# Key features turned by VectorE and moved within SBUF, in place of transposes on TensorE

## The chip, the cores and the metric

The kernel runs on one core of a Trainium2 chip. The metric is the device time of one execution in microseconds. Before the change three runs took 670.96 to 671.16 us, with a median of 671.12 us. One further execution was recorded by the hardware profiler; the profile's numbers come from that one.

The core has five engines that run side by side, each through its own queue and in that queue's order: TensorE (PE in the profile; its weight loads are listed as PEld), VectorE (DVE), ScalarE (ACT), GpSimd (POOL) and SyncE (SP). SyncE and GpSimd issue the DMAs here. Data lie in SBUF, and TensorE's results in PSUM, which has eight banks.

## The reference

A sequence of 2048 rows of width 448 is normalised (`xn`) and goes two ways; the result is `x + A(xn) + B(xn)`. B is a gated feed-forward layer with 1792 inner columns. A is attention with 16 heads of width 28, in four blocks of 512 rows, with a memory that is carried from block to block:

```python
for s in range(N):                                   # N = 4 blocks
    qs, ks, vs = q[:, :, s], k[:, :, s], v[:, :, s]
    p = _softmax(qs @ ks^T * scale + mask)           # within the block
    a_dot = p @ vs
    pq = phi(qs)                                     # phi(t) = t + 1 if t > 0 else exp(t)
    o = g * (pq @ M) / (pq @ z + 1e-6) + (1 - g) * a_dot
    pk = phi(ks)
    M = M + pk^T @ vs                                # per head, 28 x 28
    z = z + sum of pk over the rows
```

So the answer that the memory gives to a block's queries needs the key features (`pk`) and values of all blocks before it. The memory after the last block isn't needed.

## The kernel before, in words

The program has a front and a main part. The front, up to about 140 us, normalises the rows and computes keys, queries, values and the memory's answers, block by block. The main part runs feed-forward products on TensorE with the attention of 16 units woven between them, and then the output projection.

Within the front each block `b` does the following.

- *Values.* Four products `pv`, one for each 128 rows (`values`, L400; eleven matmuls of 448 columns each). ScalarE copies each into the tile `vst` (`store_values`, L395), where each head has 28 columns of values and 4 columns of ones; the ones give `z`. After the fourth, `vst` is stored to DRAM (`vd`).
- *Seven key and query steps* (`keys_queries`, L407): the 896 columns of keys and queries lie in seven chunks of 128, the keys in chunks 0 to 3 (the fourth has 64 of keys and 64 of queries). Eleven matmuls make `pp`, with features in the partitions and the block's 512 rows in the columns. ScalarE copies it to `qk` and makes two activations into the feature tile `e`; VectorE makes the low part of `qk` and finishes `e` (L424). SyncE stores `qk` to DRAM (`qd`, L420) and, from the fourth chunk on in blocks 1 to 3, the query features `e` to DRAM (`fd`, L427). The tiles `e` come from a ring of four (`bufs=4`).
- *Key features by row* (`key_rows`, L430): the update sums over rows, so it needs rows in the partitions. TensorE transposes each key chunk of `e` in four pieces into `pk`, and ScalarE copies it to `kn`. This stands after the fourth step (chunks 0 and 1) and after the sixth (chunks 2 and 3).
- *The update* (`update`, L438), right after the seventh step: for each head and each of four groups of 128 rows a matmul with 28 columns of `kn` stationary and 32 columns of `vst` streaming, added up in the bank `pmm`. Four heads at a time use four column strips of the array. Four VectorE operations add the sums to the memory `mst`. Blocks 0, 1 and 2 make an update.

In blocks 2 and 3 the answers to the queries of the block before are made. `load_features` (L459, four DMAs) brings the query features back from `fd` into the tile `phi`, of which there is one. `recall` (L462) multiplies the memory with them; this stands inside the first step in block 2 and inside the second in block 3. VectorE turns the result into a work tile `ts`: in block 2 that is `phi` itself, in block 3 `kn`. Then `answer` (L475), once for each of four groups, makes four VectorE operations and a DMA on GpSimd's queue. In block 2 the answers stand in steps 2, 3, 4 and 7.

Rows of blocks 2 and 3 are normalised by VectorE (`normalise`, L348) during the values of the block before, turned in pieces of 32 by 32 into a staging place (`stage_of`: the room of `phi` for block 2, of `acc[2]` for block 3), and sent to their partitions by 16 DMAs (`spread`, L368, half on SyncE and half on GpSimd). `split_strips` (L377) then makes operands of them in steps 3 to 6.

PSUM banks come from small rings by tag: two "p", two "s", one "m", two "gu", one "pd" (L124). Both the values and the even chunks of keys and queries use "p"; a new tile takes the bank of the one before last and waits until it has been read.

The order of TensorE, ScalarE and VectorE in the front is the order of the code (`manual_schedule(engines=FRONT)`). The queues of SyncE and GpSimd are put in order by a planner, which issues what its own estimate says is ready, and by the order of the code among what is ready.

## Time and profile before

| | |
|---|---|
| median of three runs | 671.12 us |
| profiled execution, its own time | 671.5 us |
| its span (first to last instruction) | 669.6 us |
| PE busy | 663.7 us, 99% of the span |
| DVE busy | 571.4 us, 85% |
| ACT busy | 336.1 us, 50% |
| POOL busy | 147.4 us, 22% |
| chain that ended last | PE 97%, DVE 2% |
| transposes of key features (pk, L434) | 48 |
| update products (pmm, L445), two passes each | 384 passes |

The granted clock of TensorE was full in the whole span. A row of a group reads: line, engine, operation, what it writes and reads, form, count, then total busy time and mean duration in ns of one, then the idle time before it and what ended it. A row of the timeline reads: start, duration, engine, line, operation, and in brackets idle time before it with what ended it. Matmuls are pipelined, so a row's duration overlaps the next row; what an instruction holds of TensorE's queue is read from one start to the next. For SyncE (SPq) a row is the issuing of a DMA, not its transfer.

### The profile page before, as it was taken

Reading aid. Unit: us, or ns where it says so; the run is one execution under the profiler, and the core shown is the slowest. Engines: PE = TensorE matmul, PEld = TensorE weight load, DVE = VectorE, ACT = ScalarE, POOL = GpSimd, SP = SyncE. Lnnn points to the kernel's source line nnn. Section 1 sums busy time; section 2 is a strip of 40 time slices with the busy share of each in tenths; the row PEclk is TensorE's granted clock in tenths of the full one; section 3 lists DMA queues with packets and bytes.
Section 4 is the critical chain, followed back from the end, with each engine's and each line's share of the span. In section 5 each row is a group of like instructions: output and inputs, shape, how many; then the busy total and the mean of one; then the engine's idle time right before and its main releaser. Section 6 shows DMA issues by size and latency. Waiting matters only on the chain.

```text
span 669.6 us, 11201 instructions
## 1 busy us (share of the span) xinstructions
PE 663.7 (99%) x3922; PEld 553.2 (83%) x3922; DVE 571.4 (85%) x987; ACT 336.1 (50%) x560; POOL 147.4 (22%) x354
## 2 busy tenths in 40 slices
PE   8999999999999999999999999999999999999997
PEld 7888888778888888788787878788887887888897
DVE  6986695878999899899998999899998997999864
ACT  4848474423556455455645546455544644545220
POOL 3502210002222222233122322222122122321000
PEclk9999999999999999999999999999999999999999
DMA  8537788995523432324243423426243352323442
GB/s 321 221 128 251 238 287 284 309 273 197 144 73 88 109 93 73 103 57 105 74 96 103 89 72 57 128 52 141 57 103 64 92 115 57 86 78 80 112 153 97
DMA packets 48767, 88.09 MB, mean 132 GB/s; under 512 B 6856, under 2 KB 22856, under 8 KB 48200
## 3 DMA queue, kind: packets, MB, share of 16 engines
q1 hardware_dynamic: 45048, 79.01, 39.1%
q0 software_dynamic: 3520, 8.26, 6.1%
q8 instruction: 31, 0.51, 0.3%
q14 instruction: 24, 0.20, 0.1%
q10 hardware_dynamic: 144, 0.11, 0.0%
HBM read 52.89 MB, written 32.64 MB: 128 GB/s over the span
## 4 chain that ended last, share of the span: by engine, by line
PE 97%; DVE 2%; DMA 0%; ACT 0%; issue 0%; DVEq 0%
PE pgu L260 42%; PE pd L184 21%; PE pp L412 11%; PE st L704 6%; PE pa L790 5%; PE po L889 5%; PE pv L392 5%; PE pk L434 1%; PE pmm L445 1%; PE n L467 1%; DMA acc<-in_x 0%; DVE stats L324 0%; PE pt L103 0%; DVE xn L350 0%; DVE xs L110 0%
## 5 line engine op out<-in xcount | busy, mean ns | idle before, releaser
L260 PE MATMUL pgu<-xs,wgu 128*128 128x512 f32 x1232 | 301.2, 392 | 0.0
L260 PEld LDWEIGHTS pgu<-xs,wgu 128*128 128x128 f32 x1232 | 228.7, 188 | 46.6 <-issue 2.5
L184 PE MATMUL pd<-wdn,hh 128*128 128x448 f32 x672 | 155.3, 366 | 0.0
L184 PEld LDWEIGHTS pd<-wdn,hh 128*128 128x128 f32 x672 | 122.7, 188 | 11.6 <-issue 0.8
L719 POOL TENSOR_SCALAR_AFFINE_SELECT w<-w 128x256 f32<-128x256 f32 (+1 forms) x160 | 76.1, 479 | 224.0 <-ACT w L708 157.6
L772 ACT ACTIVATE w<-w 128x1024 f32<-128x1024 f32 (+1 forms) x96 | 87.8, 915 | 58.3 <-DVE w L768 58.1
L708 ACT ACTIVATE w<-st 128x512 f32<-128x512 f32 x128 | 75.6, 592 | 60.1 <-PE st L704 59.8
L768 DVE TENSOR_TENSOR w<-w,mb 128x1024 f32<-128x1024 f32 (+1 forms) x96 | 100.6, 1054 | 0.8
L726 DVE TRANSPOSE_TENSOR_REDUCE mx<-w 128x32 f32<-128x1024 f32 x64 | 78.9, 1233 | 4.9 <-POOL w L719 4.9
L412 PE MATMUL pp<-xs,wqk 128*128 128x512 f32 x308 | 73.7, 393 | 0.2 <-DVE kn L473 0.2
L186 DVE TENSOR_TENSOR acc<-pd,acc 128x448 f32<-128x448 f32 x112 | 67.4, 602 | 4.0 <-PE pd L184 4.0
L283 ACT ACTIVATE hh<-sg 128x512 fp32r<-128x512 f32 x56 | 35.3, 631 | 67.7 <-DVE sg L277 44.6
L412 PEld LDWEIGHTS pp<-xs,wqk 128*128 128x128 f32 x308 | 57.2, 188 | 12.9 <-issue 0.8
L704 PE MATMUL st<-qk 84*128 84x128 f32 (+3 forms) x256 | 62.0, 313 | 0.0
L267 ACT ACTIVATE sg<-pgu 128x512 f32<-128x512 f32 x56 | 33.2, 592 | 45.0 <-PE pgu L260 44.9
L704 PEld LDWEIGHTS st<-qk 84*128 84x128 f32 x256 | 47.9, 189 | 8.7 <-issue 1.4
L277 DVE SCALAR_TENSOR_TENSOR sg<-sg,pgu 128x512 f32<-128x512 f32 x56 | 37.7, 673 | 10.1 <-PE pgu L260 9.9
L754 DVE STREAM_TRANSPOSE mb<-top 128x1024 f32<-128x1024 f32 x32 | 39.5, 1234 | 3.3 <-POOL top L751 3.2
L286 DVE SCALAR_TENSOR_TENSOR hh<-sg,hh 128x512 fp32r<-128x512 f32 x56 | 38.2, 681 | 0.2 <-ACT hh L283 0.2
L419 DVE TENSOR_TENSOR qk<-pp,qk 128x512 fp32r<-128x512 f32 x28 | 19.2, 686 | 22.2 <-ACT e L417 21.6
L790 PE MATMUL pa<-w,vv 128*32 128x128 f32 (+3 forms) x512 | 37.8, 436 | 0.0
L392 PE MATMUL pv<-wv,xs 128*128 128x448 f32 x176 | 37.4, 367 | 0.3 <-POOL wv L508 0.2
(113 smaller groups left out, 607.2 us busy)
## 6 DMA issues: line engine op xcount, KB each, us to landing
qk<-qd SPq DMA_DIRECT2D x192, 112.0 KB
qd<-qk SPq DMA_DIRECT2D x28, 512.0 KB
raw<-in_w_ffn SPq DMA_DIRECT2D x14, 512.0 KB
acc<-in_x SPq DMA_DIRECT2D x5, 896.0 KB
vd<-vst SPq DMA_DIRECT2D x4, 1024.0 KB
vv<-vd SPq DMA_DIRECT2D x16, 256.0 KB
od<-w POOLq DMA_DIRECT2D x16, 256.0 KB, 4.1
sums<-od SPq DMA_DIRECT2D x32, 128.0 KB
```

Of the source, the lines that this page charges most:

```text
L184: T.matmul(pd[:, :D], l, r, start=n == 0, stop=n == len(mms) - 1)
L186: V.tensor_add(acc[b][:, t, :], pd[:, :D], acc[b][:, t, :])
L260: T.matmul(dst, wgu[f][:, w, side * P:(side + 1) * P], xs[b][:, a, :], start=n == 0, stop=n == len(TERMS) - 1)
L392: T.matmul(pv[:, :D], xs[b][:, a, t * P:(t + 1) * P], wv[w], start=n == 0, stop=n == len(TERMS) - 1)
L412: T.matmul(pp, wqk[c][:, w, :], xs[b][:, a, :], start=n == 0, stop=n == len(TERMS) - 1)
L704: T.matmul(st[:, at:at + L - kb * P], self.qk[:KS, 1, h, kb * P:(kb + 1) * P], self.qk[:KS, 0, h, kb * P:], start=True, stop=True)
L708: A.activation(w, st, AF.Copy)
L719: G.affine_select(d, d, pattern=pattern, base=0, channel_multiplier=-1, compare_op=ALU.is_ge, fill=MASK)
L726: V.tensor_reduce(self.mx[:, 32 * h:32 * h + 32], w3[:, h, :2 * L].rearrange("p (b n) -> p b n", n=32), axis=mybir.AxisListType.X, op=ALU. ...
L768: V.tensor_sub(w, w, m)
L772: A.activation(w, w, AF.Exp, scale=SCALE)
L790: T.matmul(pa[32 * j:32 * j + 32, kb * P:], self.vv[:, kb, 32 * j:32 * j + 32], self.pairs[j // 2].block(j % 2, kb), start=kb == 0, stop=k ...
```

## The change

In blocks 1 and 2 the key features are no longer transposed by TensorE. VectorE transposes each 32 by 32 piece where it is (`turn_keys`), into a staging place, and 24 DMAs within SBUF carry the pieces to their partitions in `kn` (`send_keys`). The staging place is that of the next block's rows: the room of `phi` in block 1, `acc[2]` in block 2. The fourth chunk, of which only half is keys, is turned into another tile of the ring "e". Chunk 0 is turned in step 2, chunks 1 and 2 in step 3, with 16 DMAs after them, and the fourth in step 4, with 8. Block 0 keeps its transposes.

The updates of blocks 1 and 2 move into the next block, after its second value product. The first two value products wait with their copies to `vst` until the update has read it, and the third uses a bank "s".

The update's operands change places in all blocks: `vst` (32 columns) is stationary, and `kn` streams. In blocks 1 and 2 `kn` is laid out in pieces of 32 features, so that a head of 28 features streams one piece or two: 32 or 64 columns. The memory is kept transposed in a new tile `memory`, with six VectorE operations and a transpose into `mst` per update.

In block 2 only the first answer to block 1's queries stays, in step 2. The other three move into block 3, one after each of its first three value products. `phi` is loaded for block 3 after the fourth value product, no longer at the block's start.

```diff
+EXCHANGED = (1, 2)
...
         def values(b, t):
-            pv = bank("pv", "p")
+            late_update = b - 1 in EXCHANGED
+            pv = bank("pv", "s" if late_update and t == 2 else "p")
             value_terms(b, t, pv, EARLY[1] if b == 0 else TERMS)
-            store_values(b, t, pv)
+            waiting.append((b, t, pv))
+            if late_update and t == 0:
+                return
+            if late_update and t == 1:
+                update(b - 1)
+            while waiting:
+                store_values(*waiting.pop(0))
...
+        def turned(b, c):
+            space = stages[b + 1].rearrange("p (c n) -> p c n", n=256)
+            return space[:, 2 * c:2 * c + 2, :].rearrange("p c n -> p (c n)")
+
+        def turn_keys(e, et):
+            rows = et.shape[0]
+            V.transpose(et.rearrange("p (q t r) -> p t q r", q=4, t=NT),
+                        e[:rows].rearrange("p (t q n) -> p t q n", q=4, t=NT))
+
+        def send_keys(b, et=None):
+            to = kn_blocks.rearrange("p m t r -> p m (t r)")
+            src = stages[b + 1][:, :3 * L].rearrange("p (c q n) -> p c q n", c=3, q=4)
+            for q in range(4):
+                for i in range(4 if et is None else 2):
+                    queue = nc.sync if i % 2 else nc.gpsimd
+                    strip = slice(32 * i, 32 * i + 32)
+                    if et is None:
+                        queue.dma_start(to[32 * q:32 * q + 32, i:12:4, :], src[strip, :, q, :])
+                    else:
+                        queue.dma_start(to[32 * q:32 * q + 32, 12 + i, :], et[strip, P * q:P * (q + 1)])
+
+        def exchange(b, c, e):
+            if c == 1:
+                turn_keys(e[0], turned(b, 0))
+            elif c == 2:
+                turn_keys(e[1], turned(b, 1))
+                turn_keys(e[2], turned(b, 2))
+                send_keys(b)
+            elif c == 3:
+                et = sb.tile([P, L], F32, name="e", bufs=4)
+                turn_keys(e[3], et[:64])
+                send_keys(b, et)
...
-                        T.matmul(pmm[32 * i:32 * i + DH, 32 * j:32 * j + 32], kn[:, t, DH * h:DH * (h + 1)],
-                                 vst[:, t, h, :], start=t == 0, stop=t == NT - 1)
+                        m, at = divmod(DH * h, 32)
+                        if b in EXCHANGED:
+                            rows = kn_blocks[:, m:m + (1 if at < 5 else 2), t, :]
+                            at = 0
+                        else:
+                            rows = kn[:, t, DH * h:DH * (h + 1)]
+                        n = rows.shape[1] * (rows.shape[2] if len(rows.shape) > 2 else 1)
+                        T.matmul(pmm[32 * i:32 * i + 32, 64 * j + at:64 * j + at + n], vst[:, t, h, :], rows,
+                                 start=t == 0, stop=t == NT - 1)
...
+            V.transpose(mst[(b + 1) % 2].rearrange("p j c -> p (j c)"), memory.rearrange("p j c -> p (j c)"))
...
-            if b > 1:
+            if b == 2:
                 phi = features()
...
+                if last and t < 3:
+                    answer(1, t + 1, ts)
+                if last and t == 3:
+                    phi = features()
+                    for i in range(NG):
+                        load_features(2, i, phi)
...
-                if b == 2 and 0 < n < NG or last and 0 < n <= NG:
-                    answer(b - 1, n - 1, ts)
-                if b == 2 and k == 6:
-                    answer(1, NG - 1, ts)
+                if b == 2 and n == 1:
+                    answer(1, 0, ts)
+                if last and 0 < n <= NG:
+                    answer(2, n - 1, ts)
...
-                if k in (3, 5):
+                if b in EXCHANGED:
+                    exchange(b, c, e)
+                elif k in (3, 5):
                     for c in (k - 3, k - 2):
                         key_rows(c, e[c])
-                if k == 6:
+                if k == 6 and b not in EXCHANGED:
                     update(b)
```

More of the change, by code (lines that the diff above doesn't have):

```diff
@@ L315 @@
         one = sb.tile([P, 1], F32, name="one", bufs=1)
+        memory = sb.tile([P, HG, 32], F32, name="memory", bufs=1)
         kn = eight_k(F32, "kn").rearrange("p (t a) n -> p t (a n)", t=NT)
+        kn_blocks = kn.rearrange("p t n -> p (t n)")[:, :NT * D].rearrange("p (m t r) -> p m t r", t=NT, r=32)
         def statistics(b, t0, steps):
@@ L398, in store_values @@
                 nc.sync.dma_start(vd[b], vst.rearrange("p t h d -> p t (h d)"))
+        waiting = []
         def values(b, t):
-            pv = bank("pv", "p")
+            late_update = b - 1 in EXCHANGED
+            pv = bank("pv", "s" if late_update and t == 2 else "p")
             value_terms(b, t, pv, EARLY[1] if b == 0 else TERMS)
-            store_values(b, t, pv)
+            waiting.append((b, t, pv))
[5 more added lines that the diff above has]
+                store_values(*waiting.pop(0))
         stored, stages = {}, {}
@@ L444, in update @@
                         h = HG * i + j
-                        T.matmul(pmm[32 * i:32 * i + DH, 32 * j:32 * j + 32], kn[:, t, DH * h:DH * (h + 1)],
-                                 vst[:, t, h, :], start=t == 0, stop=t == NT - 1)
-            p3 = pmm[:, :P].rearrange("p (j c) -> p j c", c=32)
-            new, old = mst[(b + 1) % 2], mst[b % 2]
-            for i in range(NG):
-                strip = slice(32 * i, 32 * i + DH)
-                if b == 0:
-                    V.tensor_copy(new[strip], p3[strip])
-                else:
-                    V.tensor_add(new[strip], p3[strip], old[strip])
+                        m, at = divmod(DH * h, 32)
[7 more added lines that the diff above has]
+                                 start=t == 0, stop=t == NT - 1)
+            for i in range(NG):
+                strip = slice(32 * i, 32 * i + 32)
+                starts = [64 * j + DH * (HG * i + j) % 32 for j in range(HG)]
+                for j0, j1 in ((0, 1), (1, HG)) if i % 2 == 0 else ((0, HG),):
+                    step = starts[j1 - 1] - starts[j1 - 2] if j1 > j0 + 1 else 1
+                    at = starts[j0]
+                    new = pmm[strip, at:at + step * (j1 - j0)] if j1 > j0 + 1 else pmm[strip, at:at + DH]
+                    new = new.rearrange("p (j r) -> p j r", j=j1 - j0)[:, :, :DH]
+                    old = memory[strip, j0:j1, :DH]
+                    if b == 0:
+                        V.tensor_copy(old, new)
+                    else:
+                        V.tensor_add(old, new, old)
+            V.transpose(mst[(b + 1) % 2].rearrange("p j c -> p (j c)"), memory.rearrange("p j c -> p (j c)"))
         def features():
@@ L605, in recalled @@
                     turn_back(n2, ts, range(2))
-                n2, ts = [], kn if last else phi if b > 1 else None
+                n2, ts = [], kn if last else phi
                 n = k - (1 if last else 0)
@@ L621 @@
                     if b == 0:
+                        V.memset(memory, 0.0)
                         A.activation(gate, gate, AF.Exp, scale=-1.0)
```

## The prediction, on record before the changed kernel was built

> **What bounds the kernel now.** First the page: which engine is busy, and along which engine the chain of waits runs.
>
> ```profile
> span 669.6 us, 11201 instructions
> PE 663.7 (99%) x3922; PEld 553.2 (83%) x3922; DVE 571.4 (85%) x987; ACT 336.1 (50%) x560; POOL 147.4 (22%) x354
> PE 97%; DVE 2%; DMA 0%; ACT 0%; issue 0%; DVEq 0%
> ```
>
> TensorE has hardly a gap and carries 97% of the chain, so time taken from its queue comes off the end, and every microsecond in which it waits is added to the end. The profiled execution took 671.5 us around this span; the three runs have a median of 671.12 us, 0.4 below it. I make the sum against the profiled execution and move its result onto the median.
>
> Second, the stretches that the change touches: block 1 (its seven key and query steps, the update, and the values of block 2), block 2 in the same way, and block 3's steps. Columns: start and end, length, busy time of PE, PEld, DVE, ACT, POOL, granted clock, DMA share, GB/s.
>
> ```profile
> 51.11:80.69 29.58, 29.58 (x266) 25.46 (x265) 20.02 (x37) 19.77 (x36) 3.36 (x7) 1.00 0.73 250
> 80.69:111.58 30.89, 30.89 (x299) 25.69 (x297) 22.87 (x43) 19.05 (x34) 6.12 (x12) 1.00 0.85 288
> 111.58:140.18 28.60, 28.40 (x172) 20.64 (x170) 19.90 (x36) 12.21 (x21) 2.16 (x4) 1.00 0.88 304
> ```
>
> TensorE is busy in every microsecond of the first two, at full clock, while VectorE has 8 to 10 us free in each and the DMA engines are 73 to 88% taken. Here is TensorE's order in them.
>
> ```profile
> 61.11 1.03 PE L434 MATMUL pk<-ident,e 128*128 128x128 f32 x8
> 61.90 5.26 PE L412 MATMUL pp<-xs,wqk 128*128 128x512 f32 x22
> 67.01 1.03 PE L434 MATMUL pk<-ident,e 128*128 128x128 f32 x8
> 67.80 2.77 PE L412 MATMUL pp<-xs,wqk 128*128 128x512 f32 x11
> 70.49 1.29 PE L445 MATMUL pmm<-vst,kn 128*28 128x32 f32 x128
> 71.71 9.14 PE L392 MATMUL pv<-wv,xs 128*128 128x448 f32 x44
> ...
> 92.07 1.03 PE L434 MATMUL pk<-ident,e 128*128 128x128 f32 x8
> 92.86 5.26 PE L412 MATMUL pp<-xs,wqk 128*128 128x512 f32 x22
> 97.96 1.03 PE L434 MATMUL pk<-ident,e 128*128 128x128 f32 x8
> 98.75 2.77 PE L412 MATMUL pp<-xs,wqk 128*128 128x512 f32 x11
> 101.45 1.28 PE L445 MATMUL pmm<-vst,kn 128*28 128x32 f32 x128
> 102.66 9.08 PE L392 MATMUL pv<-wv,xs 128*128 128x448 f32 x44
> ```
>
> From one start to the next, a key and query step takes 2.55 us, a value product 2.24 (a quarter of 71.71 to 80.69, where the second window begins) and the update 1.22.
>
> **Transposes removed.** Blocks 1 and 2 lose four stretches of eight transposes. Each holds TensorE's queue for 0.79 us (61.11 to 61.90; likewise 67.01, 92.07, 97.96): -3.16 us. The four copies per block on ScalarE go too, which nothing waited for.
>
> **The update's new shape.** Values are now stationary and keys stream. The 192 products stay, as two passes each, but in blocks 1 and 2 twelve of sixteen heads cross a border of 32 features and stream 64 columns instead of 32. No row has 64 columns; the nearest are the 32-wide products of the attention, and the old update itself.
>
> ```profile
> L790 PE MATMUL pa<-w,vv 128*32 128x512 f32 x128 | 17.0, 605 | 0.0
> L790 PE MATMUL pa<-w,vv 128*32 128x128 f32 x128 | 6.4, 273 | 0.0
> L445 PE MATMUL pmm<-vst,kn 128*28 128x32 f32 x384 | 3.9, 197 | 0.0
> L473 DVE STREAM_TRANSPOSE kn<-n 128x512 f32<-128x512 f32 x8 | 5.1, 685 | 0.0
> ```
>
> From 128 to 512 columns one takes 332 ns longer: 0.865 ns a column. Four column strips of the array run side by side, so each strip passes 32 times per update, 24 of them wide: 24 x 32 x 0.865 = 0.66 us more per update. From below the price is 0: the 1.22 us are 38 ns a pass where 32 columns need 28, so something else sets part of the pace. From above, if every group of four waits for its widest, it is 0.89. I take 0.66, since column count explains three quarters of the present pace: +1.3 us for two updates (0 to 1.8). Block 0 streams 28 instead of 32, at most -0.1, left out.
>
> [...]
>
> Net work on TensorE: -1.9 us (-3.2 to -1.4). More copying out (seven VectorE operations per update where there were four) falls into VectorE's free time named above.
>
> **The wait that the new order makes: the ring of feature tiles.** A step's feature tile "e" comes from a ring of four. So far the seventh step took the tile of the third, freed by transposes. Now the fourth step's turned half takes a tile as well, so the seventh step must take the tile that the fourth step filled, and that one is free only when its store to DRAM (fd) has landed. In SyncE's queue that store stands behind eight of the new transfers, which become ready before it. SyncE's order isn't written out by hand but follows readiness (below a load at 70.40 overtakes stores that stand before it in the code), so I expect them in front. Rows of block 1:
>
> ```profile
> 60.60 0.69 DVE L424 SCALAR_TENSOR_TENSOR e<-pp,e 128x512 f32<-128x512 f32 x1
> ...
> 71.09 0.59 ACT L417 ACTIVATE e<-pp 128x512 f32<-128x512 f32 x1
> 72.38 0.69 DVE L424 SCALAR_TENSOR_TENSOR e<-pp,e 128x512 f32<-128x512 f32 x1
> ```
> ```profile
> 49.08 6.01 SPq L374 DMA_DIRECT2D stage<-phi  x8
> 67.21 0.32 SPq L427 DMA_DIRECT2D fd<-e  x1
> 70.40 0.36 SPq L460 DMA_DIRECT2D phi<-fd  x1
> SPq L460 <- DMA fd<-e: 0.9, 1, 0.9
> L374 SPq DMA_DIRECT2D stage<-phi x8: 597/604/1312, 49.1 to 53.8; - x8
> DMA to landing us min/median/max: 2.1/2.6/3.2
> ```
>
> The third step's features are ready at 61.29; two turns at 685 ns make it 62.65. Eight transfers of the same build as the spread of normalised rows (32 partitions, 512-byte pieces) take SyncE 4.8 us at 0.60 each, 6.0 as measured there. They carry a little less, so I take 5.4: SyncE is free at 68.1. The fourth step's query store goes first (0.32), its fd store at 68.45. A 256 KB fd store took 3.1 us to land (issued at 67.21, its reader released at 70.36). This one has half the bytes; I take 2.6, the spread's median: landed at 71.05.
>
> Without the transposes the seventh step ends at 70.49 - 1.58 = 68.9, and ScalarE wants the tile 0.6 later, at 69.5. It gets it 1.55 late. From that activation's start to the end of VectorE's row are 1.98 us (71.09 to 73.07), so the bank is free at 73.05. The ring of "p" banks has two: the second value product of block 2 takes the seventh step's bank. It could start at 68.9 + 2.24 = 71.15, because the update no longer stands ahead of it: a stall of 1.9 us. Bounds: 0.4, the stall that is left even with no wait for the tile (68.9 + 2.58 = 71.5), and 4.9 (7.3 us of issuing, 3.7 of landing). Everything behind that product on TensorE waits as well.
>
> The update then wants the last keys. GpSimd's twelve issues at 0.56 end at 69.4 and land by 73.8 if they take 4.4; with the stall the update begins at 75.3. They are hidden; without the stall the update would begin at 73.4 and they would cost 0.4.
>
> **Block 2, the same wait and larger.**
>
> ```profile
> 78.62 0.99 DVE L359 STREAM_TRANSPOSE acc<-xn 128x448 f32<-128x448 f32 x1
> 81.87 7.30 SPq L374 DMA_DIRECT2D stage<-acc  x8
> 89.67 0.17 DVE L143 TENSOR_SCALAR rc<-phi 128x16 f32<-128x16 f32 x1
> 90.88 0.71 DVE L478 STREAM_TRANSPOSE tb<-phi 128x512 f32<-128x512 f32 x1
> 91.49 0.64 ACT L380 ACTIVATE xs<-stage 128x512 fp32r<-128x512 f32 x1
> ```
>
> The update now stands among block 3's normalisations, which hold VectorE until 79.6 today. It ends near 77.2, its seven operations at 79.2, the three normalisations left (4.05 us) at 83.2. The spread of block 3 goes out from 83.3 over 6 to 7.3 us and lands within 2.3 (89.17 to 91.49), at 91.6 to 92.9. The first turn overwrites what the spread reads, so it waits for that; the one answer kept in its step (1.92 us, 89.67 to 91.59, now ending near 92.6) covers nearly all of it. First turn to 93.4, the third step's two operations to 94.7, two turns to 96.05, eight issues to 101.5, the fd store at 101.8, landed at 104.4. TensorE's seventh step ends at 81.7 + 20.76 - 1.58 = 100.9, ScalarE wants the tile at 101.5, 2.9 before that, and the second value product stalls for 3.3 us (0.4 to 6.5).
>
> **The answers moved.** Three answers of 1.9 us leave VectorE's block 2 and fill its idle time in block 3. Their stores leave GpSimd later, which nothing near reads. But they read "phi", and the features for the next recall are loaded into it after the last of them.
>
> ```profile
> 105.94 3.83 SPq L460 DMA_DIRECT2D phi<-fd  x4
> 116.68 1.27 PE L467 MATMUL n<-phi,mst 28*32 28x512 f32 x32
> ```
>
> Today the loads end 7 us ahead of the recall. By the times above the update ends at 110.5, its seven operations at 112.5, the last two answers at 116.3; four issues (1.3 to 3.8 us) and 2.6 to land make 120.2 to 122.7, against a recall wanted at 115.0 + 5.1 = 120.1. I take +0.5 (0 to 2.5).
>
> **Sum.** -3.16 + 1.3 + 1.9 + 3.3 + 0.5 = +3.9 us: 675.4 for the profiled execution, 675.0 on the median. Lowest stalls that still show the tile's wait (0.9 and 1.5) give about 671.6, long ones 679; that is this case's own range. A measurement of this kernel can tell about 0.2%, 1.3 us, from no change.
>
> **Rivals.** First, the store isn't late. It decides at the ring: if the eight transfers leave SyncE within 3.9 us (0.48 each), or the store stands ahead of them, the tile is free by 69.5 and only the bank's 0.4 is left at each boundary: -1.9 + 0.8 = -1.1, 670.0. For it: the tail of the spread's issues (1312 ns) may be back pressure that block 1 lacks. Against it: 604 ns is the median.
>
> Second, ending faster for certain: the store isn't late and the wider update is free, because the 38 ns are a fixed step: -3.16 + 0.8 = -2.4, 668.7. For it: the 10 ns that columns don't explain; against it: the 0.865 ns a column in the attention's products. [...]
>
> Third, DMA saturation: shares of 0.85 and 0.88 leave little for another 1.8 MB in short pieces. If the keys of block 2 land 3 us late as well and the phi loads slip by 2: 680.
>
> **How the numbers follow.** Forecast 0.48 (of it 0.03 within 0.2%); first rival 0.22 (0.14 within, 0.08 faster); second 0.20, faster; third 0.10, slower. Faster 0.28, within 0.2% 0.17, slower 0.55. The range, 668.8 to 679.0, leaves out the fastest half of the second rival and the third.
>
> **What would show it.** Right: in the rows by line ScalarE's first feature activation waits for an fd store twice; TensorE is idle before the second value product of blocks 2 and 3 by 2 and 3 us; SyncE issues eight key transfers just ahead of the fourth step's stores. Wrong: no gap there. The pmm rows tell the update's price (1.9 us between starts, or 1.2), the gap before the third recall the moved answers'. If TensorE stays gapless from 51 to 140 us, the forecast falls.

## The result, and the profile after

After the change the median of four runs is 687.46 us (686.46 to 689.19), against 671.14 us (670.96 to 671.6) for the kernel before on the same chip: a ratio of 1.0245, with a 95% interval of 1.0223 to 1.0266. The kernel became 16.3 us slower. The direction was forecast, the size was not: the forecast was +3.9 us, and the time lies above the range.

The page of the profile after; its own execution took 687.7 us.

```profile
span 685.9 us, 11246 instructions
PE 669.3 (98%) x3890; PEld 554.7 (81%) x3890; DVE 577.7 (84%) x1005; ACT 332.7 (49%) x552; POOL 161.5 (24%) x378
```

TensorE is busy 5.6 us longer than before, although it has less to do, and idle some 11 us longer. Both come from the stretches that the change touches: from 50.9 us on TensorE falls behind, and the last recall of the front is followed by feed-forward products from 156.4 us on, against 140.2 before. These 16.2 us are the whole loss. By block, measured as the length from the first key and query step to that of the next block: block 1 +4.7 us, block 2 +4.95, block 3 +6.8.

First the two stalls that were forecast. TensorE's timeline, with the idle time before a row and what ended it in brackets, and ScalarE's:

```profile
73.69 4.48 PE L395 MATMUL pv<-wv,xs 128*128 128x448 f32 x11 [2.97 <-DVE e L436]
...
110.84 3.77 PE L395 MATMUL pv<-wv,xs 128*128 128x448 f32 x11 [4.13 <-DVE e L436]
```
```profile
71.65 0.60 ACT L429 ACTIVATE e<-pp 128x512 f32<-128x512 f32 x1 [2.51 <-DMA fd<-e]
...
108.80 0.60 ACT L429 ACTIVATE e<-pp 128x512 f32<-128x512 f32 x1 [4.01 <-DMA fd<-e]
```

The second value products of blocks 2 and 3 wait, because ScalarE waits for the fourth step's store before it may write the seventh step's tile "e". SyncE's queue shows the order that was expected, eight key transfers (kn<-phi) ahead of that store; and, further on, what issues the features for block 3's recall:

```profile
62.32 5.14 SPq L469 DMA_DIRECT2D kn<-phi  x8
...
68.19 0.51 SPq L439 DMA_DIRECT2D fd<-e  x1
...
105.55 0.49 SPq L439 DMA_DIRECT2D fd<-e  x1
...
121.74 0.32 SPq L401 DMA_DIRECT2D vd<-vst  x1
122.23 3.77 SPq L520 DMA_DIRECT2D phi<-fd  x4
```

Then what was not forecast. Windows of the same trace; the columns are as in the prediction, the granted clock stands after the five engines' busy times:

```profile
50.89:68.34 17.45, 17.45 (x78) 14.45 (x77) 13.89 (x28) 14.61 (x26) 8.66 (x17) 1.00 0.77 243
...
73.69:78.09 4.40, 4.40 (x11) 3.48 (x11) 1.35 (x2) 0.00 (x0) 0.00 (x0) 0.50 1.01 386
...
114.54:116.46 1.92, 1.92 (x129) 1.83 (x129) 0.00 (x0) 0.19 (x1) 0.44 (x1) 1.00 0.97 363
```
```profile
72.71:79.54 6.83, 5.85 (x73) 4.93 (x75) 2.33 (x4) 0.20 (x1) 0.00 (x0) 0.50 0.99 366
110.26:113.67 3.41, 2.83 (x8) 2.53 (x9) 3.05 (x6) 0.75 (x1) 0.00 (x0) 0.50 1.01 392
130.74:137.56 6.82, 6.78 (x29) 3.29 (x26) 2.73 (x4) 0.00 (x0) 0.00 (x0) 0.50 0.90 341
```

In three stretches of this execution TensorE was granted half its clock. Before the change it had the full clock throughout. The value product after the first gap takes 4.40 us instead of 2.24. The four executions have mean granted clocks of 0.984 to 0.990; the stretches are known for the profiled one alone.

The third stretch belongs to block 3's recall, wanted at 126.08 (a first step of 5.1 us from 120.98). The row of its products says little of it, since a product's end is modelled; the weight loads of the same products are short and show when each group of eight was let go:

```profile
128.07 0.18 PEld L527 LDWEIGHTS n<-phi,mst 28*32 28x32 f32 x8 [2.37 <-ACT e L430]
129.76 0.18 PEld L527 LDWEIGHTS n<-phi,mst 28*32 28x32 f32 x8 [1.50 <-issue]
130.88 0.20 PEld L527 LDWEIGHTS n<-phi,mst 28*32 28x32 f32 x8 [0.94 <-DMA phi<-fd]
132.03 0.19 PEld L527 LDWEIGHTS n<-phi,mst 28*32 28x32 f32 x8 [0.95 <-DMA phi<-fd]
```

Each group needs one of the four loads of features, and the groups are let go one after the other until 132.0, six microseconds after the last load was issued (122.23 + 3.77 = 126.0). I take the release of a group that waits for its load as that load's landing. So the recall takes 7.8 us (126.08 to 133.89) where it took 1.2.

### The profile page after: what moved, and what is told of

Same layout as the page of the kernel before. It is cut to its first block, busy times and chain, and to the rows that moved or that the text cites. A ratio compares the mean times of both kernels' runs of the same rounds, so it can differ in the third digit from the quotient of the medians.

```text
span 685.9 us, 11246 instructions
## 1 busy us (share of the span) xinstructions
PE 669.3 (98%) x3890; PEld 554.7 (81%) x3890; DVE 577.7 (84%) x1005; ACT 332.7 (49%) x552; POOL 161.5 (24%) x378
## 4 chain that ended last, share of the span: by engine, by line
PE 92%; DVE 3%; DMA 3%; ACT 1%; issue 1%; DVEq 0%; SPq 0%; ACTq 0%
PE pgu L261 41%; PE pd L185 20%; PE pp L424 7%; PE st L773 6%; PE pa L859 5%; PE po L958 5%; PE pv L395 5%; DMA phi<-fd 1%; DMA fd<-e 1%; PE pmm L499 1%; PE n L527 1%; DVE e L436 1%; DVE qk L431 0%; ACT e L429 0%; DMA qd<-qk 0%
## 5 line engine op out<-in xcount | busy, mean ns | idle before, releaser
L424 PEld LDWEIGHTS pp<-xs,wqk 128*128 128x128 f32 x308 | 58.3, 190 | 12.8 <-issue 0.8
L395 PE MATMUL pv<-wv,xs 128*128 128x448 f32 x176 | 41.9, 392 | 7.5 <-DVE e L436 7.1
L395 PEld LDWEIGHTS pv<-wv,xs 128*128 128x128 f32 x176 | 34.7, 203 | 12.4 <-DVE e L436 7.8
```

Source lines behind the costliest of these rows:

```text
L395: T.matmul(pv[:, :D], xs[b][:, a, t * P:(t + 1) * P], wv[w], start=n == 0, stop=n == len(TERMS) - 1)
L424: T.matmul(pp, wqk[c][:, w, :], xs[b][:, a, :], start=n == 0, stop=n == len(TERMS) - 1)
```

## The experiments

Three theories stood at the start. *Theory 1:* the store behind the key transfers makes the stalls, and with it gone most of the loss goes. *Theory 2:* the half clock is a consequence of the gaps. *Theory 3:* the moved answers make block 3's loads late. Edits are against the kernel after, unless it is said otherwise.

### e1: the turned half has a tile of its own

```diff
-                et = sb.tile([P, L], F32, name="e", bufs=4)
+                et = two_k("et")
```

> The changed kernel, but the fourth step's turned keys go into a tile of another ring (2 KB tiles that nothing uses then), so that the seventh step's feature tile is again the one of the third step. Everything else is as in the changed kernel. Theory 1 (the fd store, standing behind eight key transfers in SyncE's queue, holds the ring of four feature tiles): ScalarE waits for no fd store in the seventh steps; TensorE's gaps before the second value products of blocks 2 and 3 shrink from 3.0 and 4.1 us to 0.4 each, and the half clock behind them goes; about 676 us (675 to 678). Rival (VectorE's additional work, or the keys landing late, makes the gaps): they stay within 1 us of what they were, 685 to 688 us.

Measured: 683.98 us (681.63 to 684.3), ratio 1.018 [1.0162, 1.0198].

```profile
71.34 2.48 PE L395 MATMUL pv<-wv,xs 128*128 128x448 f32 x11 [0.36 <-DVE e L436]
...
84.95 2.12 PE L527 MATMUL n<-phi,mst 28*32 28x512 f32 x16 [0.27 <-DMA phi<-fd]
...
107.72 2.49 PE L395 MATMUL pv<-wv,xs 128*128 128x448 f32 x11 [0.49 <-DVE e L436]
```
```profile
76.98 5.09 SPq L520 DMA_DIRECT2D phi<-fd  x4
```
```profile
86.06:92.88 6.82, 6.82 (x22) 4.63 (x15) 3.11 (x5) 0.79 (x2) 0.67 (x2) 0.50 0.78 239
```

The gaps close to 0.4 and 0.5 us, the bank's wait that the prediction left there. But only 3.5 us come back, where some 11 were expected. Block 3's late loads are still there: from its first step to the products after the last recall it takes 35.9 us (116.59 to 152.47), 7.3 more than before the change. And with the stall gone, block 2's recall comes sooner, and now it waits for its own features: SyncE issues their loads from 76.98 to 82.07, behind twelve key transfers and the stores that these held back. That recall takes 4.2 us (82.81 to 86.99), and 6.8 us at half clock begin before its end. The stall had been hiding a second price of the same backlog.

### e2: the ring stays, the key transfers go behind the store

In the code the sixteen main transfers stand in the fourth step, after its stores. The planner keeps to that only in part: in block 1 three of SyncE's eight still go ahead of the store, which is issued at 65.06 us instead of 68.19.

```diff
-                send_keys(b)
             elif c == 3:
                 et = sb.tile([P, L], F32, name="e", bufs=4)
                 turn_keys(e[3], et[:64])
+                send_keys(b)
                 send_keys(b, et)
```

> The changed kernel with its ring of four feature tiles, but the 16 key transfers are issued in the fourth step instead of the third, behind that step's two stores. Theory 1: the fd store leaves SyncE near 64 us and lands by 68, before the seventh step wants the tile at 69; the two gaps of 3.0 and 4.1 us go, but the last keys land 2 to 3 us later, at about 75 us, so the update may wait 1 to 2 us per block: 676 to 680 us. Rival (the ring of four is too small whatever the order on SyncE): ScalarE waits for the tile as long as before, 686 to 688 us.

Measured: 685.06 us (683.62 to 686.58), ratio 1.0204 [1.0184, 1.0224].

```profile
71.24 2.49 PE L395 MATMUL pv<-wv,xs 128*128 128x448 f32 x11 [0.43 <-DVE e L436]
...
85.04 2.14 PE L527 MATMUL n<-phi,mst 28*32 28x512 f32 x16 [0.72 <-DMA phi<-fd]
```

The ring of four is not too small; the order on SyncE made the stall. The time missed its expectation for the same reasons as in e1: block 2's recall waits instead, and block 3's loads stay late.

### e3: the gaps are filled with work

Useless products of 128 columns fill the wait for the second value product: 14 in block 2, 20 in block 3. Nobody reads their result.

```diff
+            if late_update and t == 1:
+                fill({2: 14, 3: 20}[b])
             value_terms(b, t, pv, EARLY[1] if b == 0 else TERMS)
...
         def fill(n):
+            warm = bank("warm", "gu")
             for _ in range(n):
```

> The changed kernel with 14 and 20 products of the identity with itself on TensorE, of no use to the result, between the first and the second value product of blocks 2 and 3: about 3 and 4 us of work in the gaps. Theory 2 (the clock that TensorE is granted halves after a gap of about 3 us, and costs time of its own): the second value products take 2.24 us instead of 4.4 and 3.7, the updates 1.9, and the time falls by 4 us to about 683 us although nothing that is waited for comes earlier. Rival (the slow products are slowed by the DMA traffic, whose share is 1.0 there): they stay at 3.7 us or more, and the time stays at 687 or rises.

Measured: 684.99 us (684.45 to 685.96), ratio 1.0207 [1.019, 1.0224].

```profile
73.78:76.19 2.41, 2.41 (x13) 1.99 (x12) 1.34 (x2) 0.00 (x0) 0.00 (x0) 1.00 1.02 396
...
125.21:135.45 10.24, 9.82 (x40) 4.75 (x37) 3.34 (x5) 0.00 (x0) 0.00 (x0) 0.50 0.78 263
```

The second value product starts at nearly the same time as in the kernel after (73.78 against 73.69) and takes 2.41 us instead of 4.40, with the DMA engines as busy (1.02 and 1.01). So it was the clock that made it long, and with work in the wait the clock stayed full (1.00 in this window, and in 108.42:110.81 after the second filled wait): theory 2 holds for these waits. The same fillings stand in e11 and e12, and in their profiles too the clock is full there (1.00 in 66:120 of e11 and in 50:170 of e12). The gain of 2.5 us is smaller than expected: in the profiles blocks 1 and 2 become 3.7 us shorter (50.89 to 117.31, against 50.89 to 120.98), but block 3's recall still waits, and 10.2 us at half clock follow where 6.8 did.

### e4: the answers stay in block 2

```diff
-                if last and t < 3:
-                    answer(1, t + 1, ts)
-                if last and t == 3:
-                    phi = features()
...
+                if b == 2 and 0 < n < NG or last and 0 < n <= NG:
+                    answer(b - 1, n - 1, ts)
...
```

> The changed kernel, but with the four answers to block 1's queries where they were before the change (steps 2, 3, 4 and 7 of block 2), and the features for the next recall loaded at the start of block 3. Theory 3 (the moved answers hold phi, and its late loads stop the recall in block 3): TensorE runs through from the second step of block 3 to the recall, the third half-clock stretch goes, and 6 us are saved: about 681 us (680 to 683). Rival (VectorE in block 2 can't carry the answers and the turns): the third step's two turns and the key transfers come 2 us later or more, the gap before the second value product of block 3 grows from 4.1 us to 6 or more, and the time stays at 685 or above.

Measured: 682.31 us (682.21 to 682.64), ratio 1.0164 [1.0149, 1.0179].

```profile
73.60 2.48 PE L395 MATMUL pv<-wv,xs 128*128 128x448 f32 x11 [2.86 <-DVE e L436]
76.01 2.00 PE L499 MATMUL pmm<-kn,vst 128*32 128x32 f32 x128
...
111.92 3.68 PE L395 MATMUL pv<-wv,xs 128*128 128x448 f32 x11 [2.31 <-DVE e L436]
...
127.38 1.27 PE L527 MATMUL n<-phi,mst 28*32 28x512 f32 x32
```

Block 3's recall runs without a wait, as theory 3 has it; but VectorE now turns block 2's second and third key chunks later (14.6 us after the block's start instead of 12.8), and block 3's first two value products wait for VectorE. With that wait included, the kernel is 5.2 us faster than with the answers moved (687.46 - 682.31).

The first two rows matter for the clock. The wait before block 2's second value product is as good as that of the kernel after, 2.86 us against 2.97, and nothing fills it. Yet the product takes 2.41 us (73.60 to 76.01) and the update behind it 1.93 (to 77.94), as with the clock at 1.00 in e3 (2.41 and 1.92), where the kernel after took 4.40 and 2.54. So an idle time of 2.86 us didn't lower the clock here.

### e5: the transfers on GpSimd, the update after all values

e1's tile; 20 of the 24 transfers on GpSimd; the update behind the fourth value product, with banks for it.

```diff
-                    queue = nc.sync if i % 2 else nc.gpsimd
+                    queue = nc.sync if et is None and i == 3 else nc.gpsimd
...
-            pv = bank("pv", "s" if late_update and t == 2 else "p")
+            pv = bank("pv", ("p", "gu", "s", "s" if b == 2 else "p")[t] if late_update else "p")
...
-            if late_update and t == 0:
+            if late_update and t < NT - 1:
                 return
-            if late_update and t == 1:
+            if late_update:
                 update(b - 1)
```

> The first experiment (fourth step's turned keys in a tile of another ring) with two more edits: 20 of the 24 key transfers per block leave from GpSimd's queue and 4 from SyncE's (before: 12 and 12), and, since that makes the last keys later (GpSimd needs 11 us for 20 issues), the update stands after the fourth value product instead of the second, the four products in four banks that are free then (p, gu, s and s in block 2, p, gu, s and p in block 3). Theory 4 (SyncE's queue is the resource that runs out: its 12 further issues of 0.6 us push the stores and loads of query features back, first the store that holds the ring, then the loads for block 2's recall): block 2's recall waits for no load, TensorE runs through from 51 us to block 3's recall at full clock, and what remains is that recall's wait for the loads behind the moved answers: 672 to 678 us. Rival (the 16 DMA engines are full, whoever issues): the loads for block 2's recall stay as late as in the first experiment, with the half clock behind: 680 us or more.

Measured: 678.27 us (677.76 to 681.28), ratio 1.0116 [1.0093, 1.0138].

```profile
79.21 0.65 PE L499 MATMUL pmm<-kn,vst 128*32 128x64 f32 x32 [1.14 <-issue]
...
84.58 1.22 PE L527 MATMUL n<-phi,mst 28*32 28x512 f32 x32
...
121.86 2.21 PE L527 MATMUL n<-phi,mst 28*32 28x512 f32 x16 [2.04 <-DMA phi<-fd]
```

Block 2's recall is prompt again. Two things help: SyncE has issued its loads by 79.40 us instead of 82.07, and the recall comes 1.8 us later than in e1 (84.58 against 82.81), since the update before it waits. So SyncE's backlog isn't separated from that delay here. The update's waits, 1.14 us in the quoted row and 1.07 in a second one, are put to no releaser in the trace; late keys are the likely reason, as GpSimd issues the last of them only at 76.7 us, and its issuing stands still three times behind landings of earlier ones (3.2 us in all). Block 3's recall still waits for its loads, and some 3.4 us at half clock follow it (the mean granted clock of this execution is 0.997).

### e6: e5, with the answers late in block 2

Answers in steps 2, 5, 6 and 7 of block 2, the loads at the start of block 3.

```diff
-                if b == 2 and n == 1:
-                    answer(1, 0, ts)
+                if b == 2 and n in (1, 4, 5, 6):
+                    answer(1, max(n - 3, 0), ts)
...
```

> The fifth experiment, with the four answers to block 1's queries in steps 2, 5, 6 and 7 of block 2 and the loads for the next recall at the start of block 3, as before the change. Theories 1, 3 and 4 together: no wait of TensorE is left between 51 and 140 us, and the sum of its work alone decides: -3.16 for the transposes, +1.4 for the two updates at the 1.92 us seen at full clock, so about 669.4 us (668.5 to 670.5), faster than before the change. Rival (VectorE's block 2 is full with the turns and the answers): TensorE waits for VectorE before the values of block 3, with half clock behind it: 673 us or more.

Measured: 677.26 us (676.71 to 677.79), ratio 1.0094 [1.0077, 1.0111].

```profile
105.93 8.86 PE L395 MATMUL pv<-wv,xs 128*128 128x448 f32 x35 [3.29 <-DVE xs L387]
```

The forecast of 669.4 us failed and the rival was right: with the answers in block 2 VectorE makes the low parts of block 3's rows 3.3 us late, and some 3.4 us at half clock follow (the mean granted clock of this execution is 0.997).

### e7: the update's new form alone

No keys go the new way, and the answers stay: what is left is the exchange of the update's operands and the transposed memory.

```diff
-EXCHANGED = (1, 2)
+EXCHANGED = ()
...
```

> Of the change only the update's new form: values stationary, keys streaming (28 columns in every block), memory kept transposed; no exchange, the transposes on TensorE as before, the answers and the loads where they were before. The form alone costs nothing: 670.8 to 671.8 us. Rival (the changed roles themselves make the update slower, not the 64 columns): each of three updates takes 1.9 us instead of 1.2, 673 us.

Measured: 671.1 us (670.6 to 671.64; ten runs), ratio 0.9998 [0.9989, 1.0008]. With 28 streamed columns the update takes what it took, 1.29 us:

```profile
70.23 1.29 PE L499 MATMUL pmm<-kn,vst 128*32 128x28 f32 x128
```

### e8: the moved answers alone

As e7, but with the answers and loads where the change puts them.

> The seventh experiment plus the moved answers: three answers to block 1's queries in block 3, and the loads for its recall after the fourth value product; no exchange. Theory 3 alone (the moved answers suffice to make block 3's recall late): the answers end near 110 us, the loads go out behind the values' 1 MB store at 112 us and land after the recall wants them at 116.7: a gap of 1 to 3 us and perhaps half clock behind it, 673 to 678 us. Rival (the loads are late only because SyncE and the updates push them): no gap, 670.8 to 672 us.

Measured: 678.12 us (677.44 to 678.32), ratio 1.0102 [1.0087, 1.0117]. The answers' move alone costs 7.0 us (against e7), where I had +0.5. SyncE's queue and the recall's weight loads:

```profile
112.35 0.36 SPq L401 DMA_DIRECT2D vd<-vst  x1
112.81 2.72 SPq L520 DMA_DIRECT2D phi<-fd  x3
```
```profile
119.82 0.18 PEld L527 LDWEIGHTS n<-phi,mst 28*32 28x32 f32 x8 [3.19 <-DVE kn L533]
121.04 0.20 PEld L527 LDWEIGHTS n<-phi,mst 28*32 28x32 f32 x8 [1.04 <-DMA phi<-fd]
122.42 0.20 PEld L527 LDWEIGHTS n<-phi,mst 28*32 28x32 f32 x8 [1.18 <-DMA phi<-fd]
```

The loads are issued from 111.97 on, as soon as the last answer has left the tile, and land until 122.4, 5.9 us after the recall is wanted (116.48). A store of 1 MB (vd) is issued among them.

### e9: e8 with that store behind the loads

```diff
-            if t == NT - 1:
+            if t == NT - 1 and b < NB - 1:
                 nc.sync.dma_start(vd[b], vst.rearrange("p t h d -> p t (h d)"))
...
                         load_features(2, i, phi)
+                    nc.sync.dma_start(vd[b], vst.rearrange("p t h d -> p t (h d)"))
```

> The kernel of e8 (keys as before, answers moved) with one change: in block 3 the 1 MB store of the values is issued behind the four loads of recall features instead of among them. If the store in front of the loads is what makes them late, they land within some 4 us of their issue (from 112.0 in e8), the third recall runs without a wait of over 0.5 us, the stretch at half clock after it is gone, and the time is 671.5 to 673. The rival: the last moved answer ends at 111.9 and holds the tile until then, so that the loads come too late whatever stands among them; then the wait stays at 1 to 2.3 us, the half clock comes as in e8, and the time is 676 to 678.

Measured: 675.33 us (673.36 to 677.04), ratio 1.0055 [1.0035, 1.0076]. The six executions fall into two groups: 673.36, 673.5 and 673.74 us at mean granted clocks of 0.999 to 1.0, and 676.91, 677.03 and 677.04 us at 0.995. The median lies between the groups, and is the time of neither. The profile is of an execution of the second group.

```profile
112.05 1.67 SPq L520 DMA_DIRECT2D phi<-fd  x4
113.81 0.38 SPq L654 DMA_DIRECT2D vd<-vst  x1
```
```profile
118.48 0.15 PEld L527 LDWEIGHTS n<-phi,mst 28*32 28x32 f32 x8 [1.48 <-DMA phi<-fd]
119.67 0.20 PEld L527 LDWEIGHTS n<-phi,mst 28*32 28x32 f32 x8 [1.04 <-DMA phi<-fd]
```

All four loads are issued by 113.72, 1.8 us sooner, and still the last lands 6 us later. The rival's wait came (1.48 us before the third group). One program with two clocks also prices the half clock: 3.5 us (677.03 - 673.5). The four executions of e8 are all at 0.994 or 0.995, so e8 is to be compared with the second group: the store's place is worth 1.1 us (678.12 - 677.03). What is left at full clock, 2.4 us (673.5 - 671.1 of e7), goes with the late start of the loads. So e8's 7.0 us are some 2.4 for the late loads, 1.1 for the store among them and 3.5 for the clock; but with the store behind, the clock fell in three executions of six only. In the profiled one it fell although the products' rows show idle waits of 0.8 us in all. e11 takes that up.

### e10: one block's keys, the rest as before

Only block 1's keys go the new way, with e5's tile, banks and update; 8 of the 24 transfers are on SyncE; the answers stay.

```diff
-EXCHANGED = (1, 2)
+EXCHANGED = (1,)
...
+                    queue = nc.sync if i == (3 if et is None else 1) else nc.gpsimd
...
```

> Only the second block's keys go the new way; the third block's are transposed on TensorE as before, and the answers stay where they were. As in e5 the turned fourth piece has a tile of its own and the update stands behind the fourth value product; 8 of the 24 sends are on SyncE (4 of 16 and 4 of 8) and 16 on GpSimd. The theory that the loss is in the queues and in the half clock that follows their gaps: transposes -1.9 (their price in the kernel after), update +0.7, waits for the last keys 0 to 1.1 (e5 had 1.1 and 1.1 with 20 sends on GpSimd): -1.2 to -0.1 against the kernel before, so 670.0 to 671.2 and no stretch at half clock. The rival: eight sends on SyncE still hold back the loads for block 2's recall, which then waits and is followed by 3.4 us or more at half clock: 673 to 675.

Measured: 671.39 us (670.99 to 671.85; eleven runs) against 671.24, ratio 1.0002 [0.9993, 1.0012]: no difference, at full clock. Windows of it:

```profile
50.93:68.43 17.50, 17.50 (x78) 14.45 (x77) 13.92 (x28) 14.61 (x26) 8.64 (x16) 1.00 0.83 264
...
77.33:79.25 1.92, 1.92 (x130) 1.83 (x129) 0.00 (x0) 0.20 (x1) 0.00 (x0) 1.00 0.75 226
...
81.98:84.36 2.38, 2.38 (x34) 0.52 (x33) 1.13 (x2) 1.71 (x3) 1.33 (x3) 1.00 1.04 388
```

This is the cleanest account of the idea. The seven steps take 17.50 us instead of 19.38 (-1.88); the update takes 1.92 instead of 1.22 (+0.70); and the recall takes 2.38 instead of 1.15 (+1.2), since the last piece of its features lands late. SyncE has issued the loads by 79.86 us, 2.0 later than before the change, and the DMA engines are full during the recall (share 1.04); how much each adds isn't shown. The gain is used up to the last tenth.

### e11: e3, and block 3's wait filled too

Twelve useless products stand in front of the third recall.

```diff
                 def recalled():
+                    if last:
+                        fill(12)
                     n2.extend(recall(b - 1, phi))
```

> e3 with twelve more useless products in block 3, in front of the third recall, where TensorE waited 2.4 us for the recall's features in e3 and then ran 10.2 us at half clock. If the half clock comes from the idle time, the clock stays full from 50 us to the end, the recall takes 1.2 us after some 2.8 us of useless products, and of the 8.5 us that e3 lost between the start of that wait and the second feed-forward step about 3 stay: 679 to 681 against e3's 685.0. If something else slows the recall and what follows it (the DMA engines are all busy there), the products change nothing or add their own time: 685 or more.

Measured: 685.86 us (684.27 to 686.75), ratio 1.0222 [1.0203, 1.0241]. The expectation failed: no gain, and the half clock came as before. The weight loads show why:

```profile
125.70 0.15 PEld L529 LDWEIGHTS n<-phi,mst 28*32 28x32 f32 x8
126.78 0.18 PEld L529 LDWEIGHTS n<-phi,mst 28*32 28x32 f32 x8 [0.93 <-issue]
127.89 0.15 PEld L529 LDWEIGHTS n<-phi,mst 28*32 28x32 f32 x8 [0.93 <-DMA phi<-fd]
129.03 0.20 PEld L529 LDWEIGHTS n<-phi,mst 28*32 28x32 f32 x8 [0.99 <-DMA phi<-fd]
```
```profile
129.03:135.88 6.85, 6.85 (x20) 4.12 (x21) 1.52 (x3) 0.00 (x0) 0.00 (x0) 0.50 0.69 274
```

All four executions are at clocks of 0.994 or 0.995. The twelve products cover only the wait for the first piece. The other three land 1.1 us apart, and between them TensorE does little, although its products, 0.6 us long in the records, make it look busy. After 3.3 us of that the clock is halved.

### e12: e11, with products between the groups as well

```diff
             for i in range(NG):
+                if fill and i:
+                    fill(3)
                 for j in range(HG):
...
```

> e11 with three useless products more in front of each of the second to fourth groups of eight recall products, which in e11 started 1.1 us apart, each when its piece of the features had landed, so that TensorE did little from 125.7 us on although hardly any idle time is on record there, and ran at half clock from 129.0 to 135.9. If the clock counts what the array does and not the recorded gaps, it now stays full in block 3: the last group still starts at about 129 (the pieces land when they land), but the recall ends 1 us earlier and the two steps after it run 1.8 us shorter: 682.5 to 683.8 against e11's 685.9. The rest of the third recall's loss is then the wait for the pieces itself, some 5 us. If the clock falls for another reason (all DMA engines busy), it falls here as well, and the time is 685.5 or more.

Measured: 685.99 us (683.85 to 687.68), ratio 1.0225 [1.0196, 1.0254]. Again the executions differ in their clock: 683.85 and 684.65 us at 1.0, 687.33 and 687.68 at 0.997. The profile is of the one with 684.65 us. Its clock, from before the first stall to after the last recall:

```profile
50.00:170.00 120.00, 119.94 (x892) 97.75 (x891) 82.72 (x161) 53.29 (x93) 28.22 (x54) 1.00 0.82 259
```
```profile
131.78 0.15 PEld L531 LDWEIGHTS n<-phi,mst 28*32 28x32 f32 x8
132.77 0.77 PEld L261 LDWEIGHTS pgu<-xs,wgu 128*128 128x128 f32 x4 [0.84 <-issue]
```

Here the clock stays full in all of it, with the DMA engines taken as before (0.82 in the mean). With products between the groups the clock stayed up in two executions of four, without them (e11) in none of four. That speaks for the work that the array does as what counts, rather than gaps in the record, but two against two doesn't settle it, and no trace shows where the other two lost their clock. Even at full clock the time hardly fell, because the filling was too coarse: a group and its three products take 1.86 us, so the groups start 1.86 us apart instead of 1.1, and the recall ends 1.35 us later (132.77 - 123.44 = 9.3 us after it is wanted, against 130.90 - 122.93 = 8.0 in e11). What follows the recall, up to the end of the next one, runs 2.5 us shorter (20.66 us against 23.13): the half clock's price in that stretch.

## Why the prediction was right or wrong

**Right.** *The stalls' mechanism and place.* The fourth step's store in block 1 was put at 68.45 and issued at 68.19; in block 2 it was put 20.1 us after the block's start and issued 20.4 after (105.55 - 85.14). ScalarE waits for it twice; e2 shows that the order on SyncE alone does it. *The update's price:* 0.66 forecast, 0.70 measured (1.92 against 1.22, at full clock, in the kernel after and in e10). *The exchange of operands by itself* costs nothing (e7). *The keys are hidden behind the stall* in the kernel after: the update follows the stalled product without a wait on record. In e1, without the stall, it starts at 73.75 us, again without one, where I had 73.4 and a cost of 0.4.

**Sizes that were off.** Per block the seven steps lost 1.93 and 1.90 us instead of 1.58, 0.7 us better than forecast in all: the price of 0.79 for eight transposes left out that the steps next to them took longer too (2.69 us from 67.80 to 70.49, where the first four steps of block 1 took 2.50 each). The stalls: the first value product and the wait behind it take 5.35 us in block 1 and 6.84 in block 2, 3.1 and 4.6 us more than a product's 2.24, where I had 1.9 and 3.3. That is 2.5 us of the miss. The step that failed is the landing: the store took 3.5 us in block 1 (68.19 to 71.65) and 3.25 in block 2, and I took 2.6, the spread's median, though the one store to DRAM in my rows had taken 3.1. That makes some 1.5 of the 2.5. The steps' earlier end makes some 0.7, for what ends sooner waits longer, and the later issue in block 2 makes 0.3. The eight transfers were no part of it: they took 5.14 us in block 1 where I had 5.4.

**The step that failed most: "I take +0.5 (0 to 2.5)" for the moved answers.** The loads' start was right: forecast at 1.3 us after the block's start, measured at 1.25 (122.23 - 120.98). Their issuing took 3.8 us, the upper end of what I had. But they land 6 us after that and not 2.6, one by one: the recall's last group is released 5.95 us after the recall is wanted, so the wait is worth some 5.7 us. e8 has the same move alone at 7.0 us, of which e9 puts some 3.5 down to the half clock and 1.1 to the order on the queue. The 2.6 us came from transfers of 48 and 64 KB within SBUF, issued between 49 and 54 us; the loads are of 224 KB from DRAM. And the window of the kernel before around those transfers has a DMA share of 0.52, where block 3's recall meets 1.0:

```profile
48.00:56.00 8.00, 8.00 (x39) 6.95 (x38) 5.55 (x17) 4.50 (x8) 4.64 (x8) 1.00 0.52 112
```

The third rival, saturation of the DMA engines with the loads late, comes nearest to these rows; it had a chance of a tenth. Its loads were late at full engines, as it said, but its late keys did not come, and that the full engines are the cause isn't shown.

**The step that was missing: what a gap does to the clock.** The half clock cost 2.2 us in the value product and 0.6 in the update of block 1 (2.54 us there against 1.92), 1.5 in block 2's value product, and in block 3 about 0.9 in the recall's last group and 1.2 in the steps after it: 6.4 us in the profiled execution. The prediction put this at nothing: its rows had all been taken at full clock. In e3's profile work in the waits before the second value products kept the clock at 1.00, and e9 shows two groups of executions of one program, 3.5 us apart, with and without the half clock. The measured stretches at half clock last 6.83, 3.41 and 6.82 us in the kernel after, 6.82 in e1 and e8, 10.24 in e3 and 6.85 in e11. How long a gap has to be for that, the runs don't say: 2.86 us left the clock full in e4, while in e5 it fell after a recall with a gap of 2.04 us, and in e11 after three waits of 0.9 us between small products.

Together: +2.5 for the stalls, +6.4 for the clock, +5.2 for the loads, -0.7 for the steps, and -1.0 because the last recall no longer waits (1.36 us instead of 2.37): 12.4, which is the miss of 16.3 against 3.9.

**The rivals.** The first, a store that isn't late, at 670.0: e1 and e2 make that case, and the time is 684 and 685. Its condition can be had, but its price was wrong. Behind the stall stood the late features of block 2's recall, which the working had not followed: their loads stand behind the same key transfers on SyncE. And it left out block 3's late loads, which e1 and e2 keep, and the clock. The second fell with the update's price.

**What stays open.** How much idle time lets the clock fall can't be read from these runs: e4's 2.86 us and e10's recall with one late piece didn't lower it, and e9's executions differ with the same code. Nor does any run show what slows the landings. The DMA share isn't shown to decide it: in e10 the last load for block 2's recall landed 3.5 us after its issue (79.86 to 83.36) at shares of 0.71 and then 1.04, in the kernel after block 3's took 6.0 at 1.03. Counted from the first issue to the last landing the four loads took 7.6 us in e9, 8.0 in e10 and 9.8 in the kernel after.

## What to carry to other kernels

When work moves from an engine to DMAs, follow the queue that issues them to the end: every later load and store on it moves back (SyncE had issued the loads for block 2's recall by 77.8 us before the change and by 82.07 in e1), and the first stall that this makes can hide a second one. Price a load that TensorE waits for with landings measured on transfers of its kind and size, at the DMA share that it will meet. And for a forecast gap on TensorE like those here (1.9 to 4.1 us), or a stretch in which it only trickles (e11), allow for the clock: 0 in e4, 1.5 to 2.8 us in the kernel after, up to 3.5 in e9. Look at the granted clock of every execution before a median is read.

## What the runs showed of the hardware

- TensorE was granted half its clock for 3.4, 6.8 or 10.2 us after most recorded waits of 1.9 to 4.1 us, but not after one of 2.86 us (e4). Waits filled with useless products left it at full clock (1.00 at the second value products in the profiles of e3, e11 and e12).
- One program can have both: three executions of e9 at 673.4 to 673.7 us with a mean clock of 0.999 to 1.0, three at 676.9 to 677.0 us with 0.995.
- A TensorE that the record calls busy can have little to do: the recall's groups of eight short products, 1.1 us apart, are recorded as 3.2 us of work in 3.3, and the clock fell all the same (e11). The weight loads show the waits: 0.15 to 0.20 us each group, with 0.93 to 0.99 us between.
- SyncE took 0.64 us to issue each of the eight larger key transfers of block 1 (5.14 for eight, 48 KB each), and about as much for the 16 KB ones (2.69 for four).
- At a DMA share of 1.01 to 1.04, loads of 224 KB in block 3 landed 1.1 to 1.7 us apart, the last 6.0 us after its issue (kernel after, e9, e11), and 6.9 with a store of 1 MB among them (e8, shares of 0.95 to 1.10).
